# Four sets of state powers and two tap products made by GpSimd instead of VectorE, with a new issue order, in a kernel of a state-space layer beside sliding attention

## The chip, the core and the metric

The kernel runs on one core of a Trainium2 chip. The core has five engines, each with its own instruction queue: TensorE (PE; its weight loads are PEld), VectorE (DVE), ScalarE (ACT), GpSimd (POOL) and SyncE (SP), which issues nearly all DMAs. Within a queue instructions run in order; between queues they wait for each other through semaphores. The metric is the device time of one execution in microseconds.

## What is computed

Two layers on separate inputs of 2048 tokens x 448 channels, their outputs side by side in 896 columns of bf16:

```python
# A: diagonal state-space layer, P = 448 complex states
Lam_bar = exp(dt * Lam);  B_bar = ((Lam_bar - 1) / Lam)[:, None] * Bmat
Bu = einsum("bld,pd->blp", x, B_bar)
for t in range(L):
    h = Lam_bar * h + Bu[:, t]
y = 2 * einsum("blp,dp->bld", hseq, Cmat).real + x * Dskip
# B: attention of 16 heads x 28 channels over W = 8 earlier tokens, 2 apart
q, k, v = split(x @ wqkv)
attn = softmax(where(mask, einsum("bhsd,bhswd->bhsw", q, kg) * Dh**-0.5, -1e9))
o = einsum("bhsw,bhswd->bhsd", attn, vg);  out = o @ wo
```

## The kernel before

**Layout.** Token 16 p + j sits in partition p at position j: every partition holds 16 consecutive tokens. What the text calls "tokens 0 to 7" are the positions j = 0 to 7 of every partition, block b = 0; positions 8 to 15 are block b = 1. Each block has two halves of four positions, r = 1 (the upper) and r = 0. Work goes from b = 1 to b = 0 and from r = 1 to r = 0.

**Part A** (class PartA). The 448 complex states are seven sets m of 64, real and imaginary parts in 128 rows. The recurrence is done as matrix products: the input products (PE, L1247 and L1256), then steps that multiply by powers of Lam_bar (PE, L1266 to L1304, a scan over chunks), then the carries back to all tokens (L1311 to L1350), each followed by an eviction from PSUM by ScalarE. The powers of one set are 15 matrices, block-diagonal, in one tile "pw" of 128 x 1920 bf16. `powers` (L1190) builds it with one product of VectorE (L1197): a mask "Dm" times the small table "spair", both spread out by broadcasting. There are four pw buffers for seven sets: set m from 4 on can be built only after the last use of set m - 4 (the unit done[m - 4], after L1350). Then the outputs: y = C h + D x (PE, L1458 and L1462), an eviction (`outputs`, L1463 on) and a DMA to the output. For the last four positions D x is made by VectorE (`load_skip`, L1439) and added in the eviction (L1474).

**Part B** (class PartB). Projections of q and k (L481, L488, L514) and of v (L753, L760); logits as products on VectorE (L654, L656, L660: tile "prods") summed over each head's channels by PE (L672, L678); softmax (L701 to L722); a DMA transposition of the attention weights. Then `pv`: for each block b and half r, four tap pairs i = 0 to 3, each a product of weights and values over 2 taps x 4 positions x 448 channels = 3584 elements on VectorE (`mul`, L819; the first straight into the sum, tile "rb", the others into the three "prods" buffers, tap pair 3 into the third), three additions (`add`, L822) and the sum of the two taps of the pair (L838, or in two parts L841 for the very last half). The sum goes through a transposition (SP, L872, or PE, L884, for the last half) to the output projection (PE, L900, L908, L915), an eviction by ScalarE and a DMA.

**Order.** The program first lists its work as 685 units (`Planner.add`): engine, cost, function, units it depends on, buffers. An entry may name two engines. `ORDER` then gives the sequence in which all units are issued, as a flat list of unit numbers, 1000 more where the unit runs on the second of its engines. If the list's length is not that of the units, the planner makes a sequence itself from costs and priorities. Each engine gets its instructions in that sequence, so `ORDER` fixes what stands behind what on every queue. The engines wait only for data and buffers, wherever a unit stands in the list.

**Units that matter here** (numbers of before): 221, 260, 299, 338, 373, 412, 449 are the power sets m = 0 to 6; 533 to 540 are `pv` for b = 1 and 571 to 579 for b = 0. In each half the four units are: products 0 and 1; product 2 and addition 1; product 3 and addition 2; addition 3 and the sum of the taps. On POOL's queue stand, after the setup, only four memsets of the first row of v's halo (L778), of 0.7 us each.

Of the kernel before, what the change touches and what calls it, by code (L numbers as in the profile page):

```python
# [10 lines left out]
ALU = mybir.AluOpType  # L11
# [7 lines left out]
NCH = 128  # L19
# [20 lines left out]
NC = 3  # L40
# [6 lines left out]
ADD = (0, 0, 0, 0, 0, 0, 0)  # L47
EADD = (0, 0, 0, 0)
# [272 lines left out]
class PartB:  # L321
# [464 lines left out]
    def pv(self, b, prio, deps):  # L786
# [13 lines left out]
        lasts, halves, trs = {}, {}, {}  # L800
        for r in (1, 0):
            last = getattr(self, "pv_last", None)
            half = getattr(self, "u_half", None)
            ahead = half is not None
            us = (5, 4, 1, 0)
            for n in range(4):

                def step(n=n, r=r, part=0, half=half):
# [4 lines left out]
                    def mul(i):  # L813
                        u = us[i]
                        o = j0 + 4 * r + DIL * u
                        w0 = 4 * (u // 4) + 2 * (u % 2)
                        aa = self.attn[b][:, w0:w0 + 2, :, r, :].rearrange("q y i h -> q (y i) h").unsqueeze(2).to_broadcast(
                            [NCH, 8, DH, H])
                        V.tensor_tensor(tmp[i].rearrange("p (j d h) -> p j d h", j=8, d=DH), aa, self.vd[:, o:o + 8], op=ALU.mult)  # L819
# [3 lines left out]
                    if n == 0:  # L823
                        mul(1 if half else 0)
                        mul(2 if half else 1)
                    elif n == 1 and half:
                        mul(3)
                        mul(0)
                    elif n == 2 and half:
                        add(1)  # L830
                        add(2)
                    elif n < 3:
                        mul(n + 1)
                        add(n)
                    elif 2 * b + r > 0:
                        add(3)
                        if not EADD[2 * b + r]:
                            V.tensor_tensor(acc[:, n1:2 * n1], acc[:, 0:n1], acc[:, n1:2 * n1], op=ALU.add)  # L838
# [4 lines left out]
                for u in us[:2 + ahead] if n == 0 else us[n + 1 + ahead:n + 2 + ahead] if n < 3 else ():  # L843
# [3 lines left out]
                cost = 2 * vec2(2 * n1) if n < 3 else vec2(2 * n1) + vec2(n1) * (not EADD[2 * b + r]) if 2 * b + r > 0 else vec2(n1)  # L847
                last = P.add("DVE", cost, step, dd + [self.u_attn[b], last, *self.u_prod[0], *self.u_prod[1], *self.u_lg[0], *self.u_lg[1],
                                         *self.u_vm, *self.u_proj, *deps, half if n == 1 else None], prio - 0.1 * r)
# [5 lines left out]
            g = 2 * b + r  # L855
            halves[g] = self.u_half = None
            if EADD[g]:

                def merge(g=g):
                    acc = self.acc[g]  # L860
                    nc.gpsimd.dma_start(acc[:, n1:2 * n1], acc[:, 0:n1], accum_op=ALU.add)
                halves[g] = self.u_half = P.add("POOL", 1.1, merge, [last], PRI["wo"], lat=3.5)
            if not hasattr(self, "u_first"):
                self.u_first = last
        for r in (1, 0):
            g = 2 * b + r
            if g > 0:
# [5 lines left out]
                trs[r] = P.add("SP", 1.7, trd, [halves[g] or lasts[r][1]], PRI["wo"], lat=3.6)  # L873
# [70 lines left out]
class PartA:  # L944
# [245 lines left out]
    def powers(self, m, prio, deps):  # L1190
# [4 lines left out]
        def build():  # L1195
            t = pool.tile([NCH, 2 * NPW, 32, 2], bf16, name="pw", tag="pw", bufs=4)
            V.tensor_tensor(t[:], self.o["Dm"][:].rearrange("p (a b) -> p a b", b=2).unsqueeze(1).to_broadcast(  # L1197
# [5 lines left out]
        u = P.add("DVE", vec2(2 * NPW * PL), build, [self.u_s, *deps], prio, acq="pw")  # L1203
        return box, u

    def scan(self, prio, qk_done):
# [9 lines left out]
        for m in range(NM):  # L1216
# [99 lines left out]
            def carry(out, lt, Sc, hv, new=False):  # L1316
                mt(out[:, 0:NCH], lhsT=lt, rhs=Sc, start=new, stop=True, **kw)
# [13 lines left out]
            def again(n, box=box, pair=pair):  # L1331
# [5 lines left out]

# [4 lines left out]
            def s6(box=box, Sc=Sc, L=L, hget=hget, again=again, add=bool(ADD[m])):  # L1342
                if add:
                    again(0)
# [254 lines left out]
```

## Time and profile before

| | |
|---|---|
| Time, two runs | 140.18 and 140.28 us, median 140.23 |
| The profiled execution | 140.0 us, of which the span from the first to the last instruction is 138.3 us |
| Granted TensorE clock, mean | 0.997 |
| VectorE, products of `pv` (L819) | 16 x 2.02 us, of them 12 into "prods" |
| VectorE, additions of `pv` (L822) | 11 x 2.02 us |
| VectorE, power sets (L1197) | 7 x 1.15 us, the first at 19.9, the last at 85.5 us |
| GpSimd, all | 69 instructions, 17.7 us; the last ends at 33.1 us |
| DMA | 16.58 MB, mean 120 GB/s |

How to read what follows: "128x3584 bf16<-128x3584 bf16" is the output and the first input, partitions x elements. In a line of the timeline stand start, duration, engine, line and operation; consecutive instructions of one line are merged ("x3"). In a line of groups stand the count, the busy time in all, the mean duration in ns, and the idle time of the engine before them with what ended it. The chain of waits follows the work that ended last back to the start; its durations run to the next step, not to the instruction's own end. An "SPq" is the issue of a DMA by SP. Durations on POOL are rough.

### The profile page before, as it was taken

To read this page: it belongs to the slowest core of one execution; us is meant where nothing else is said; L and a number is where in the kernel's file an instruction comes from. 1 tells how busy PE (TensorE), PEld (TensorE's weight loads), DVE (VectorE), ACT (ScalarE), POOL (GpSimd) and SP (SyncE) were. 2 spreads that over 40 slices of the span, in tenths; PEclk is the share of its full clock that TensorE was granted. 3 is DMA by queue.
4 is the path that set the end of the run, shared out by engine and by line. 5 is a ranking of instruction groups with operands and counts; after the bars stand their busy time and mean duration, and the time that the engine had idled before them with its cause. 6 is when DMAs were issued, how large, how long until landed. Compare 5 with 4: busy or idle time off the path is not lost.

```text
span 138.3 us, 2835 instructions
## 1 busy us (share of the span) xinstructions
PE 131.3 (95%) x1065; PEld 67.2 (49%) x1071; DVE 123.0 (89%) x134; ACT 88.3 (64%) x199; POOL 17.7 (13%) x69
## 2 busy tenths in 40 slices
PE   7999989999999999999999999999999999999790
PEld 2534334444455453656534563556565455445450
DVE  1369998899999999997999999999999999999920
ACT  3555587998554976657695998689547151721571
POOL 7589830025000000000000000000000000000000
PEclk9999999999999999999999999999999999999998
DMA  4968965658658525648899039350093425575163
GB/s 128 269 126 208 179 87 61 153 130 95 81 113 53 97 52 112 179 104 131 167 222 198 0 67 240 95 111 0 0 95 103 139 78 118 141 163 169 35 197 100
DMA packets 41694, 16.58 MB, mean 120 GB/s; under 512 B 33685, under 2 KB 41044, under 8 KB 41681
## 3 DMA queue, kind: packets, MB, share of 16 engines
q1 hardware_dynamic: 41618, 16.40, 57.6%
q8 instruction: 8, 0.13, 0.4%
q14 instruction: 5, 0.04, 0.1%
q10 hardware_dynamic: 63, 0.01, 0.0%
HBM read 4.32 MB, written 3.67 MB: 58 GB/s over the span
## 4 chain that ended last, share of the span: by engine, by line
DVE 39%; PE 38%; SPq 9%; issue 5%; ACT 3%; DMA 3%; DVEq 0%; ACTq 0%
DVE rb L822 11%; DVE prods L819 11%; SPq L366 6%; PE v_ps L760 6%; PE scb L1247 5%; DVE rb L819 4%; PE scp L1247 4%; PE logits L672 3%; DMA rb<-in_B_x_dram 3%; DVE pw L1197 2%; PE qk_ps L481 2%; DVE prods L656 2%; PE wo_ps L915 2%; DVE rb L838 2%; ACT qk L218 1%
## 5 line engine op out<-in xcount | busy, mean ns | idle before, releaser
L819 DVE TENSOR_TENSOR prods<-attn,vd 128x3584 bf16<-128x3584 bf16 x12 | 24.0, 2018 | 0.0
L822 DVE TENSOR_TENSOR rb<-rb,prods 128x3584 bf16<-128x3584 bf16 x11 | 22.2, 2019 | 0.1
L656 DVE TENSOR_TENSOR prods<-qk 128x3072 bf16<-128x3072 bf16 (+1 forms) x15 | 19.1, 1325 | 0.0
L481 PE MATMUL qk_ps<-rb 128*128 128x512 bf16 x60 | 14.4, 379 | 0.7 <-DMA rb<-in_B_x_dram 0.6
L1462 PE MATMUL y_ps<-Ccat,qk 128*128 128x448 bf16 x60 | 14.6, 352 | 0.0
L218 ACT CAST vd<-v_ps 128x448 bf16<-128x448 f32 x16 | 7.9, 540 | 5.2 <-PE v_ps L760 4.9
L1247 PEld LDWEIGHTS <-Bcat 128*128 128x128 bf16 x84 | 7.5, 100 | 7.4 <-issue 1.1
L1294 ACT CAST ubuf<-scb 128x64 bf16<-128x64 f32 x35 | 7.3, 220 | 5.9 <-PE scb L1301 3.5
L218 ACT CAST qk<-wo_ps 128x448 bf16<-128x448 f32 (+1 forms) x16 | 8.1, 529 | 4.5 <-PE wo_ps L908 2.8
L1462 PE MATMUL y_ps<-Ccat,h 128*128 128x448 bf16 x45 | 11.0, 353 | 0.0
L1247 PE MATMUL scb<-xaT_sb,Bcat 128*128 128x512 bf16 x42 | 10.9, 380 | 0.0
L218 ACT CAST qk<-y_ps 128x448 bf16<-128x448 f32 (+1 forms) x9 | 5.6, 663 | 8.2 <-issue 4.2
L760 PE MATMUL v_ps<-rb 128*128 128x448 bf16 x48 | 10.1, 353 | 0.0
L220 ACT ACTIVATE qk<-qk_ps 64x512 bf16<-64x512 f32 (+1 forms) x15 | 8.9, 599 | 1.7 <-PE qk_ps L488 1.3
L481 PEld LDWEIGHTS <-rb 128*128 128x128 bf16 x60 | 5.6, 98 | 7.8 <-issue 1.0
L660 DVE TENSOR_TENSOR prods<-qk 128x768 bf16<-128x768 bf16 (+3 forms) x18 | 9.1, 566 | 0.1
L1462 PEld LDWEIGHTS <-qk 128*128 128x128 bf16 x60 | 5.8, 98 | 5.3 <-ACT qk L1364 0.2
L819 DVE TENSOR_TENSOR rb<-attn,vd 128x3584 bf16<-128x3584 bf16 x4 | 8.1, 2021 | 0.1
L908 PE MATMUL wo_ps<-wo_p,rb 128*128 128x448 bf16 x36 | 8.1, 353 | 0.0
L1197 DVE TENSOR_TENSOR pw<-Dm,spair 128x1920 bf16<-128x1920 bf16 x7 | 8.1, 1150 | 0.0
L218 ACT CAST qk<-qk_ps 128x512 bf16<-128x512 f32 (+2 forms) x11 | 6.3, 585 | 2.5 <-PE qk_ps L488 1.1
L1247 PE MATMUL scp<-xaT_sb,Bcat 128*128 128x512 bf16 x30 | 7.8, 381 | 0.0
(197 smaller groups left out, 259.0 us busy)
## 6 DMA issues: line engine op xcount, KB each, us to landing
out_dram<-qk SPq DMA_DIRECT2D x32, 112.0 KB, 1.8
vd<-vd SPq DMA_DIRECT2D x3, 392.0 KB, 4.5
rb<-in_B_wqkv_dram SPq DMA_DIRECT2D x3, 336.0 KB, 4.5
qk<-in_A_x_dram SPq DMA_DIRECT2D x1, 448.0 KB
ra<-in_A_B_re_dram SPq DMA_DIRECT2D x1, 392.0 KB, 4.3
ra<-in_A_B_im_dram SPq DMA_DIRECT2D x1, 392.0 KB
rb<-in_A_C_re_dram SPq DMA_DIRECT2D x4, 98.0 KB, 2.9
rb<-in_A_C_im_dram SPq DMA_DIRECT2D x4, 98.0 KB, 3.5
```

The lines of the kernel that those rows point to most:

```text
L218: nc.scalar.copy(out, in_)
L220: nc.scalar.mul(out, in_, scale)
L366: nc.sync.dma_start(self.xT[:, j], bass.AP(x.tensor, x.offset + j * D - DT, [[T * D, NCH], [1, KT * NCH]]), transpose=True)
L481: nc.tensor.matmul(out(n), lhsT=w(n, full, k), rhs=self.xT[:, j:j + 4, k, :], start=(not rfirst and k == 1), stop=(rfirst and k == KT - 1) ...
L656: V.tensor_tensor(out.rearrange("p i j k q -> p i (j k) q"), qq.unsqueeze(1).to_broadcast([NCH, 2, 4 * nk, NCH]), bass.AP(kk.tensor, kk.of ...
L660: V.tensor_tensor(jk(out[:, i, a:e]), qq, kk, op=ALU.mult)
L760: nc.tensor.matmul(box["ps"][:].rearrange("p h d -> p (h d)"), lhsT=self.xT[:, j, k, :], rhs=self.wv[:, k, :], start=False, stop=(k == KT ...
L819: V.tensor_tensor(tmp[i].rearrange("p (j d h) -> p j d h", j=8, d=DH), aa, self.vd[:, o:o + 8], op=ALU.mult)
L822: V.tensor_tensor(acc, acc, tmp[i], op=ALU.add)
L1197: V.tensor_tensor(t[:], self.o["Dm"][:].rearrange("p (a b) -> p a b", b=2).unsqueeze(1).to_broadcast([NCH, 2 * NPW, 32, 2]), self.sp[:, m ...
L1247: mt(box[i], lhsT=self.Bcat[:, k, m, :], rhs=self.xk(slice(i, None, 4), k), start=(i % 2 == 0 and k == 0), stop=False, **kw)
L1462: nc.tensor.matmul(ps, lhsT=h, rhs=self.Ccat[:, m, :], start=(m == 0 and not skip), stop=(m == NM - 1), skip_group_check=True)
```

## The change

1. `powers`: the unit may run on VectorE or GpSimd. In the new `ORDER` sets 0 to 2 stay on VectorE, and 3, 4, 5 and 6 run on GpSimd.
2. `pv`: the product of tap pair 3 becomes a unit of its own (n = 4, listed ahead of the other four of its half), for VectorE or GpSimd. In the new `ORDER` the two of b = 1 stay on VectorE, the two of b = 0 run on GpSimd. Addition 3 waits for it. The other units are then: products 0 and 1; product 2 and addition 1; addition 2; addition 3 and the sum of the taps. There are four units more, 689, and the new list has 689 numbers.
3. `ORDER` is another list from the last loads of A's x on; up to there it is the same. In it, three evictions of v (positions 7, 10, 12), one copy of A's x rows (i = 2, L1005) and two evictions of y (positions 7 and 10) run on VectorE instead of ScalarE. On VectorE the skip multiply (L1439) and the first of the three L1474 now stand ahead of the last three units of `pv`; in before they stood behind them. On SP the two loads for the skip multiply stand together behind the first output of y (before: one some twenty issues ahead of the other), the fourth halo copy of v goes ahead of the transposing load of C, and the output DMAs have another sequence. On POOL two of the four memsets stay ahead of the power sets; one follows set 3, one set 6; behind that come the two tap products.
4. Two options that were off in before (sums added by DMA: `ADD`, `EADD`, with `NC`) are taken out of the code. The instructions they would have made did not exist.

```diff
-            for n in range(4):
+            for n in (4, 0, 1, 2, 3):
...
-                        V.tensor_tensor(tmp[i].rearrange("p (j d h) -> p j d h", j=8, d=DH), aa, self.vd[:, o:o + 8], op=ALU.mult)
+                        (V if eng == "DVE" else nc.gpsimd).tensor_tensor(
+                            tmp[i].rearrange("p (j d h) -> p j d h", j=8, d=DH), aa, self.vd[:, o:o + 8], op=ALU.mult)
...
                     if n == 0:
-                        mul(1 if half else 0)
-                        mul(2 if half else 1)
...
+                        mul(0)
+                        mul(1)
+                    elif n == 4:
+                        mul(3)
                     elif n < 3:
-                        mul(n + 1)
+                        if n == 1:
+                            mul(2)
                         add(n)
...
+                c = vec2(2 * n1)
+                cost = (2 * c, 2 * c, c, (c + vec2(n1)) if 2 * b + r > 0 else vec2(n1), (c, 9.8))[n]
...
+                if n == 4:
+                    third = P.add(("DVE", "POOL"), cost, lambda e, f=step: f(eng=e), dd, prio - 0.1 * r, until=0.0)
+                else:
+                    last = P.add("DVE", cost, step, dd + [third if n == 3 else None], prio - 0.1 * r)
...
-        def build():
+        def build(eng):
             t = pool.tile([NCH, 2 * NPW, 32, 2], bf16, name="pw", tag="pw", bufs=4)
-            V.tensor_tensor(t[:], self.o["Dm"][:].rearrange("p (a b) -> p a b", b=2).unsqueeze(1).to_broadcast(
+            (V if eng == "DVE" else nc.gpsimd).tensor_tensor(t[:], self.o["Dm"][:].rearrange("p (a b) -> p a b", b=2).unsqueeze(1).to_broadcast(
...
-        u = P.add("DVE", vec2(2 * NPW * PL), build, [self.u_s, *deps], prio, acq="pw")
+        u = P.add(("DVE", "POOL"), (vec2(2 * NPW * PL), 5.2), build, [self.u_s, *deps], prio, acq="pw", until=0.0)
...
 ORDER = [
...
-    145, 142, 146, 149, 144, 23, 188, 189, 125, 169, 127, 179, 490, 126, 491, 493, 505, 132, 130, 492, 485, 486,
+    145, 142, 146, 149, 144, 132, 125, 127, 188, 189, 126, 505, 515, 184, 516, 518, 506, 508, 185, 177, 519,
...
+    303, 286, 250, 251, 1338, 252, 253, 255, 257, 287, 288, 254, 292, 526, 256, 258, 215, 532, 293, 525, 305,
+    216, 307, 306, 308, 259, 1373, 289, 290, 309, 294, 296, 291, 339, 340, 341, 342, 310, 295, 297, 343, 345,
...
+    409, 544, 440, 464, 465, 441, 445, 442, 444, 466, 467, 402, 403, 404, 446, 468, 633, 469, 470, 577, 1578,
```

More of the change, by code (lines that the diff above doesn't have):

```diff
@@ L799, in pv, with step @@
         self.oTd = getattr(self, "oTd", {})
-        lasts, halves, trs = {}, {}, {}
+        lasts, trs = {}, {}
         for r in (1, 0):
             last = getattr(self, "pv_last", None)
-            half = getattr(self, "u_half", None)
-            ahead = half is not None
             us = (5, 4, 1, 0)
-            for n in range(4):
-                def step(n=n, r=r, part=0, half=half):
+            for n in (4, 0, 1, 2, 3):
+                def step(n=n, r=r, part=0, eng="DVE"):
                     alloc()
@@ L842, in pv @@
                 dd = []
-                for u in us[:2 + ahead] if n == 0 else us[n + 1 + ahead:n + 2 + ahead] if n < 3 else ():
+                for u in us[:2] if n == 0 else us[2:3] if n == 1 else us[3:] if n == 4 else ():
                     o = j0 + 4 * r + DIL * u
@@ L846, in pv @@
                         dd += self.u_vh[p] if p < HALO else [self.u_v[p - HALO]]
-                cost = 2 * vec2(2 * n1) if n < 3 else vec2(2 * n1) + vec2(n1) * (not EADD[2 * b + r]) if 2 * b + r > 0 else vec2(n1)
-                last = P.add("DVE", cost, step, dd + [self.u_attn[b], last, *self.u_prod[0], *self.u_prod[1], *self.u_lg[0], *self.u_lg[1],
-                                         *self.u_vm, *self.u_proj, *deps, half if n == 1 else None], prio - 0.1 * r)
+                c = vec2(2 * n1)
+                cost = (2 * c, 2 * c, c, (c + vec2(n1)) if 2 * b + r > 0 else vec2(n1), (c, 9.8))[n]
+                dd += [self.u_attn[b], last, *self.u_prod[0], *self.u_prod[1], *self.u_lg[0], *self.u_lg[1], *self.u_vm, *self.u_proj, *deps]
+                if n == 4:
+                    third = P.add(("DVE", "POOL"), cost, lambda e, f=step: f(eng=e), dd, prio - 0.1 * r, until=0.0)
+                else:
+                    last = P.add("DVE", cost, step, dd + [third if n == 3 else None], prio - 0.1 * r)
             lasts[r] = [last, last]
@@ L1314, in ev3, with carry @@
                 nc.scalar.copy(hget()[:, 3, 0:384], box[3][:, 0:384])
-            def carry(out, lt, Sc, hv, new=False):
-                mt(out[:, 0:NCH], lhsT=lt, rhs=Sc, start=new, stop=True, **kw)
+            def carry(out, lt, Sc, hv):
+                mt(out[:, 0:NCH], lhsT=lt, rhs=Sc, start=False, stop=True, **kw)
                 mt(out[:, NCH:512], lhsT=lt, rhs=hv[:, 3, 0:384], start=False, stop=True, **kw)
@@ L1329, in ev1f, with back @@
                 nc.scalar.copy(hget()[:, 1, :], box[1])
-            def again(n, box=box, pair=pair):
+            def back(n, box=box, pair=pair, hget=hget):
                 if pair and n == 0:
@@ L1403, in scan @@
             b0 = b2 = eh
-            add = bool(ADD[m])
-            if not hold[0] and not add:
+            if not hold[0]:
                 b0 = P.add("PE", pe(1, 512), lambda f=back: f(0), [b0], PRI["bk"] + m * 0.1, acq="W" if pair else "s")
-            if not hold[pair ^ 1] and not add:
+            if not hold[pair ^ 1]:
                 b2 = P.add("PE", pe(1, 512), lambda f=back: f(1), [b2, b0], PRI["bk"] + m * 0.1, acq=None if pair else "s")
-            v0 = P.add("PE", pe(2, 256), s6, [b0, u3], pc, acq=("W" if pair else "s", "cP") if add else None)
-            v2 = P.add("PE", pe(1, 512), s7, [b2, u1, v0 if add and pair else None], pc, acq="s" if add and not pair else None)
+            v0 = P.add("PE", pe(2, 256), s6, [b0, u3], pc)
+            v2 = P.add("PE", pe(1, 512), s7, [b2, u1], pc)
             if pair:
```

52 lines of the change are left out of this document (11 added, 41 removed), and 45 rows, old and new, of the table ORDER.

## The prediction

> **What bounds the kernel now.** I read the page first, then the windows, then VectorE's timeline and the chain, and last GpSimd's rows, since the change moves work from the one to the other.
>
> ```profile
> PE 131.3 (95%) x1065; PEld 67.2 (49%) x1071; DVE 123.0 (89%) x134; ACT 88.3 (64%) x199; POOL 17.7 (13%) x69
> POOL 7589830025000000000000000000000000000000
> DVE 39%; PE 38%; SPq 9%; issue 5%; ACT 3%; DMA 3%; DVEq 0%; ACTq 0%
> ```
>
> Two engines share the chain about evenly, and POOL does nothing after the tenth of 40 slices. The windows (busy time of PE, PEld, DVE, ACT and POOL in each stretch) show whether the two take turns or are full together:
>
> ```profile
> 18.00:44.00 26.00, 25.60 (x263) 12.61 (x264) 24.69 (x33) 19.80 (x39) 3.41 (x6) 1.00 0.65 101
> 64.00:80.00 16.00, 15.76 (x108) 8.02 (x109) 15.93 (x10) 12.73 (x36) 0.00 (x0) 1.00 0.72 142
> 90.00:126.00 36.00, 35.90 (x255) 19.69 (x256) 35.79 (x20) 19.43 (x44) 0.00 (x0) 1.00 0.45 100
> 128.50:138.30 9.80, 5.54 (x45) 3.30 (x45) 3.59 (x6) 4.99 (x10) 0.00 (x0) 0.96 0.37 117
> ```
>
> From 90 to 126 us PE is busy 35.90 and VectorE 35.79 of 36 us. Neither has room: what lengthens VectorE's work there lengthens the kernel, and what shortens it alone meets a full PE. The profiled execution took 140.0 us, 1.7 more than its span of 138.3, and 0.23 under the median of 140.23; I count against 140.0.
>
> **The change part by part.** *Removed from VectorE.* Four power sets (m = 3 to 6) and the last product of r = 1 and of r = 0 for tokens 0 to 7. Their rows in VectorE's timeline, and in the chain (which counts start to start, so without the overlap with the next instruction):
>
> ```profile
> 49.41 1.15 DVE L1197 TENSOR_TENSOR pw<-Dm,spair 128x1920 bf16<-128x1920 bf16 x1
> 68.52 1.15 DVE L1197 TENSOR_TENSOR pw<-Dm,spair 128x1920 bf16<-128x1920 bf16 x1
> 80.58 1.15 DVE L1197 TENSOR_TENSOR pw<-Dm,spair 128x1920 bf16<-128x1920 bf16 x1
> 85.52 1.15 DVE L1197 TENSOR_TENSOR pw<-Dm,spair 128x1920 bf16<-128x1920 bf16 x1
> 107.58 2.02 DVE L819 TENSOR_TENSOR prods<-attn,vd 128x3584 bf16<-128x3584 bf16 x1
> 122.50 2.02 DVE L819 TENSOR_TENSOR prods<-attn,vd 128x3584 bf16<-128x3584 bf16 x1
> 85.60 1.07 DVE pw L1197
> 83.67 1.94 DVE prods L819
> ```
>
> 4 x 1.07 + 2 x 1.94 = 8.2 us less on VectorE.
>
> *Added to GpSimd.* No such size ran there. Its nearest rows are products of two float32 operands:
>
> ```profile
> L1081 POOL TENSOR_TENSOR karg<-kv,arg 128x105 f32<-128x105 f32 x1 | 0.4, 362 | 0.0
> L1124 POOL TENSOR_TENSOR cs<-sh 128x210 f32<-128x210 f32 x1 | 0.5, 539 | 0.0
> ```
>
> 105 elements more cost 177 ns, 1.69 ns each. So 1920 elements take 3.2 us and 3584 take 6.0 us, beside about 0.2 us of fixed cost: 4 x 3.2 + 2 x 6.0 = 24.8 us. The lower end is half of it (bf16 is half the bytes): 12.4 us. The upper end is the price that the code's planner has for the two, 5.2 and 9.8 us: 40.4 us. I take 24.8, the only one with a measured slope behind it.
>
> *Do the two engines run beside each other?* This decides the sign. In the only place where a GpSimd instruction that reads SBUF met one of the large products of VectorE:
>
> ```profile
> L1129 POOL TENSOR_SCALAR la<-la,turn x2: 499/788/1078, 14.3 to 14.8; 128x7 f32<-128x7 f32 x2
> 14.31 1.57 POOL L1129 TENSOR_SCALAR la<-la,turn 128x7 f32<-128x7 f32 x2
> 14.36 0.29 DVE L222 COPY rb<-rb 64x512 bf16<-64x512 bf16 x1
> 14.68 0.96 DVE L654 TENSOR_TENSOR prods<-qk 128x1536 bf16<-128x1536 bf16 x1
> L1127 POOL TENSOR_TENSOR la<-cs,ex 128x14 f32<-128x14 f32 x1 | 0.2, 238 | 0.1
> ```
>
> Twice the same 7 elements: 499 and 1078 ns, where 14 elements took 238 ns just before. The first ends at 14.81, 0.16 after VectorE's copy (14.65); the second at 15.88, 0.24 after VectorE's product (15.64). Both look as if GpSimd stood still until VectorE had finished. If so the two exclude each other, and it matters little who goes first: a GpSimd product of 3.2 us needs 3.2 us in which VectorE runs no product, and between 90 and 126 us VectorE leaves 0.2 us free. For the other direction there is only a hint: of three small products of VectorE beside GpSimd work, the one that began 0.03 us after a GpSimd instruction took 0.12 us longer than its like, and another was not slowed at all:
>
> ```profile
> 8.01 0.15 DVE L1108 TENSOR_TENSOR t<-pf 128x7 f32<-128x7 f32 x1
> 8.16 0.50 POOL L1086 TENSOR_SCALAR kf<-kf 128x105 f32<-128x105 f32 x1
> 8.19 0.27 DVE L1109 TENSOR_TENSOR den<-den,t 128x7 f32<-128x7 f32 x1
> 8.75 0.50 POOL L1091 TENSOR_SCALAR kc<-kf 128x105 f32<-128x105 f32 x1
> 8.93 0.17 DVE L1114 TENSOR_TENSOR ll<-pf,rden 128x14 f32<-128x14 f32 x1
> ```
>
> The Trainium skill speaks against this change: "SBUF — State Buffer", section "Who interferes with whom", has a VectorE instruction with two SBUF inputs and a GpSimd instruction that reads SBUF exclude each other, the one that starts first holding the port for the whole instruction. By that rule the sum is the one I make below. The trace agrees for VectorE's hold (1078 ns above); no row shows GpSimd's.
>
> The skill's "GPSIMD Engine Reference", section 3.1, gives 4497 ns for a float32 product of 2048 elements, at which the six would take about 4 x 4.2 + 2 x 7.9 = 32.6 us (an estimate from that page), and the sum below would be 7.8 us more.
>
> So on VectorE: 24.8 added less 8.2 removed, **+16.6 us**; ends 12.4 - 8.2 = +4.2 and 40.4 - 8.2 = +32.2; and -8.2 if the two do not disturb each other at all.
>
> *Evictions moved from ScalarE to VectorE*: three of v's (j = 7, 10, 12) and the copy of A's x rows for i = 2; two of y's (j = 7, 10) come at the very end.
>
> ```profile
> L222 DVE CAST qk<-qk_ps 128x512 bf16<-128x512 f32 (+1 forms) x9 | 6.1, 688 | 0.5 <-POOL kc L1093 0.3
> L222 DVE COPY rb<-rb 64x512 bf16<-64x512 bf16 (+1 forms) x3 | 0.8, 268 | 0.9 <-DMA rb<-in_B_wqkv_dram 0.8
> ```
>
> 448 of 512 columns: 0.60 us, so 3 x 0.60 + 0.27 = **+2.1 us** on a full VectorE. ScalarE, at 64%, gains nothing that counts.
>
> *The tail.* After the last adds of tokens 0 to 3 the chain now runs:
>
> ```profile
> 127.49 1.10 DVE rb L841
> 129.49 0.45 PE pt_o L884 x8
> 130.32 1.62 DVE qk L1474 x2
> 131.98 0.61 PE pt_o L884 x8
> 132.59 2.28 PE wo_ps L915 x12
> 134.94 0.53 ACT qk L218
> ```
>
> The new order puts the skip multiply (L1439) and the first of the three L1474 ahead of the last adds; two L1474 still follow. The stretch of the chain that hangs on L1474, from 129.94 (where L884 x8 ends) to 131.98, can go: **-2.0 us**; at worst 0.
>
> *Waits and queues.* PE's first product with a GpSimd set (L1266) waits for GpSimd, with all of PE's queue behind it. There is room:
>
> ```profile
> 64.75 0.38 PE L1350 MATMUL scp<-h,pw 128*128 128x512 bf16 x1
> 76.79 0.40 PE L1266 MATMUL scb<-qk,pw 128*128 128x512 bf16 x1
> 30.32 2.82 POOL L778 MEMSET vd<- 1x896 f32 x4 [11.68 <-ACT qk L218]
> ```
>
> Set 4 takes set 0's buffer, free after 64.75, and is needed at 76.79: 12 us for a product of 3.2 (5.2 at most). Set 3 needs no buffer and starts behind two of the four memsets, near 30.32 + 1.4 = 31.7. VectorE's third addition (L822) waits for the last product; behind it on VectorE stand the half sums, and for them wait SP's transposition (L872) and PE's output projection. The buffer comes free with the previous block's third addition; from there to its own there are a half sum and five 1.94 us steps, 10.8 us: room for 6.0, barely for 9.8. The memset left behind set 6 (halo rows 2 to 5) and the other transfers that change places on SP's queue have POOL's and SP's idle time around them: nothing.
>
> *Sum.* 140.0 + 16.6 + 2.1 - 2.0 = 156.7. Set 3 falls where PE, not VectorE, carries the chain:
>
> ```profile
> 35.30 2.38 PE v_ps L760 x12
> 39.43 2.38 PE v_ps L760 x12
> ```
>
> so I count its net 3.2 - 1.07 = 2.1 us as half hidden: **forecast 155.6 us**. This case's own ends are 144 (12.4 us of GpSimd work) and 172 (40.4 us).
>
> **The rivals.** *They run side by side, and PE bounds.* For it: L1114 above, and that GpSimd is idle when it gets the work. Against it: L1129. VectorE would be 8.2 - 2.1 = 6.1 us shorter, but PE can only close its own gaps: 0.8 us between 128.5 and 134.9 (5.54 busy of 6.4; after that there is only eviction and output), 0.1 from 90 to 126, 0.2 from 64 to 80, 0.4 from 18 to 44, and as much again in gaps that the modelled matmul ends cover. That is 1.5 to 3 us: 137 to 138.5. It decides if GpSimd's products leave VectorE's steps at 1.94 us. The little that lies beyond 2% needs nearly all of these gaps.
>
> *They share the port finely.* GpSimd reads bf16 in pairs and takes only 12.4 us from VectorE: 140.0 + 4.2 + 2.1 - 2.0 = 144. For it: half the bytes per element. Against it: the whole-instruction wait of L1129.
>
> *VectorE always wins, GpSimd starves.* Then set 4 to 6 come late and PE stops; the six products still need their 24.8 us of free port, so it ends near the forecast, with the stops on PE instead.
>
> That the order list is not used is excluded: 685 + 4 new units are 689, as many as it has numbers.
>
> **How the numbers follow.** They exclude each other, either winner: 0.45, 155.6 us. Fine sharing: 0.15, 144. Side by side: 0.40, 137 to 138.5 and in part up to 140, of which 0.15 beyond 2%. A measurement of this kernel tells about 2% (2.8 us) from no change. Faster 0.15; same 0.25; slower 0.45 + 0.15 = 0.60. The range 137 to 163 leaves out some 0.10 below and 0.10 above (GpSimd at the planner's price). Within the likeliest case alone it is 146 to 163.
>
> **What would show it.** Right: VectorE's steps at L819 and L822 near GpSimd's six products grow from 2.0 to 5 us or more, or GpSimd's products last 5 us or more and end just behind a VectorE instruction; VectorE's busy time grows, PE's windows from 64 us on fall below 90%. Wrong: L819 and L822 keep 2.02 us in all their rows while GpSimd's L1197 runs; VectorE's busy time falls to about 117 us and PE's share rises. The eviction term is wrong if ScalarE, not VectorE, ends the waits before 60 us; the tail term if L1474 still stands between L841 and the last L884.

## The result and the profile after

| | before | after |
|---|---|---|
| Time, median of two runs | 140.23 us | 166.45 us (166.12 and 166.78) |
| Ratio to before, 95% interval | | 1.187 (1.177 to 1.197) |
| Span of the profiled execution | 138.3 us | 165.0 us |
| Last adds of tokens 0 to 3 end, by VectorE's timeline | 128.57 us | 153.29 us |

The kernel became 18.7% slower: slower as forecast, but 10.9 us beyond the forecast of 155.6 and 3.5 us beyond the upper end of the range. Lines have moved in the code: `powers` is now L1185, the products of `pv` are L814, its additions L818, the half sums L830 and L833, the skip multiply L1409, the sums with y L1444.

The page after, busy time of the engines:

```profile
PE 140.6 (85%) x1065; PEld 69.7 (42%) x1071; DVE 145.0 (88%) x134; ACT 86.0 (52%) x193; POOL 48.9 (30%) x75
```

VectorE was relieved of six products and yet is busy 22 us longer, at the same share of a longer span. Which of its instructions grew is in the groups by line and shape (count, then busy time and mean ns of one):

```profile
L814 DVE TENSOR_TENSOR prods<-attn,vd 128x3584 bf16<-128x3584 bf16 x10 | 29.5, 2980 | 0.0
L814 DVE TENSOR_TENSOR rb<-attn,vd 128x3584 bf16<-128x3584 bf16 x4 | 21.3, 5324 | 0.1
L818 DVE TENSOR_TENSOR rb<-rb,prods 128x3584 bf16<-128x3584 bf16 x11 | 22.2, 2019 | 0.3
```

The products' means hide a few very long ones; the additions (L818) still take 2.02 us. VectorE's timeline after (start, duration) shows them, each where a GpSimd product runs:

```profile
30.09 10.09 DVE L653 TENSOR_TENSOR prods<-qk 128x3072 bf16<-128x3072 bf16 x5
41.29 0.62 DVE L219 CAST vd<-v_ps 128x448 bf16<-128x448 f32 x1 [1.10 <-PE v_ps L757]
...
72.72 10.37 DVE L814 TENSOR_TENSOR prods<-attn,vd 128x3584 bf16<-128x3584 bf16 x2
...
87.00 5.26 DVE L814 TENSOR_TENSOR prods<-attn,vd 128x3584 bf16<-128x3584 bf16 x1
...
111.54 1.09 DVE L830 TENSOR_TENSOR rb<-rb 128x1792 bf16<-128x1792 bf16 x1
112.67 8.65 DVE L814 TENSOR_TENSOR rb<-attn,vd 128x3584 bf16<-128x3584 bf16 x1
...
132.47 8.61 DVE L814 TENSOR_TENSOR rb<-attn,vd 128x3584 bf16<-128x3584 bf16 x1
...
146.81 1.08 DVE L1409 TENSOR_TENSOR qk<-qk,rb 128x1792 bf16<-128x1792 bf16 x1
148.08 1.09 DVE L1444 TENSOR_TENSOR qk<-y_ps,qk 128x896 bf16<-128x896 f32 x1 [0.19 <-issue]
149.08 2.02 DVE L818 TENSOR_TENSOR rb<-rb,prods 128x3584 bf16<-128x3584 bf16 x1
151.20 2.09 DVE L833 TENSOR_TENSOR rb<-rb,prods 128x1792 bf16<-128x1792 bf16 x2
```

GpSimd's timeline, the same stretches:

```profile
32.30 3.39 POOL L1185 TENSOR_TENSOR pw<-Dm,spair 128x1920 bf16<-128x1920 bf16 x1
...
71.47 4.60 POOL L1185 TENSOR_TENSOR pw<-Dm,spair 128x1920 bf16<-128x1920 bf16 x1 [34.99 <-PE scp L1331]
...
111.64 7.79 POOL L814 TENSOR_TENSOR prods<-attn,vd 128x3584 bf16<-128x3584 bf16 x1 [20.49 <-DVE rb L818]
131.39 7.81 POOL L814 TENSOR_TENSOR prods<-attn,vd 128x3584 bf16<-128x3584 bf16 x1 [11.95 <-DVE rb L818]
```

Read the first tap product. GpSimd's record starts at 111.64, while VectorE's half sum runs until 112.63. GpSimd ends at 119.43. VectorE's next product is in hand from 112.67 and ends at 121.32; it needs 2.02 us, so it ran from 119.30. Read so, GpSimd stood 1.0 us until VectorE's instruction was over, then held VectorE for 6.7 us, and it got its turn ahead of a VectorE instruction that followed at once. The sets bear this out: the record of set 4 (from 71.47, 4.60 us) is 1.2 us longer than that of set 6 (from 86.98, 3.41 us), and VectorE's instruction that was running then had 1.34 us to go for set 4 (until 72.81) and 0.10 us for set 6 (until 87.08). The two engines take turns, one instruction at a time.

The windows after (busy time of PE, PEld, DVE, ACT and POOL in each stretch, then granted clock) show what this did to TensorE, which had been nearly full up to 126 us:

```profile
31.00:44.00 13.00, 9.46 (x104) 4.02 (x103) 11.86 (x11) 4.19 (x9) 5.42 (x5) 0.74 0.48 91
80.00:100.00 20.00, 12.61 (x97) 6.54 (x96) 19.79 (x11) 9.51 (x30) 5.39 (x3) 0.82 0.26 54
150.00:165.00 15.00, 11.57 (x76) 6.34 (x74) 5.77 (x8) 5.47 (x10) 0.00 (x0) 0.84 0.43 138
```

TensorE's longest wait is for no product at all, but for a 0.15 us cast of the skip weights, which VectorE reached only at 97.30 us, behind the holds of sets 4 to 6 (85.30 us in run e1_order below, where TensorE does not wait for it):

```profile
PE scb L1244 <- DVE dsk L1054: 7.1, 1, 7.1
```

**The account, by VectorE's timeline.** Stretch: set 3 3.8 us (10.09 against 6.29 for the same five products in run e2_taps below), sets 4 and 5 6.4 (10.37 against 3.95), set 6 3.2 (5.26 against 2.02), the two tap products 6.6 each (8.65 and 8.61 against 2.02): 26.7 us. Removed products: -8.2. Three evictions of v and a copy ahead of the last adds: +2.1. The skip multiply and one sum with y, now ahead of the last two steps (146.81 to 149.08): +2.3. Together 22.9 of the 24.7 us by which the last adds end later; the other 1.8 were not followed one by one, but the 1.10 us for TensorE at 41.29, behind set 3, is among them. From the last adds to the end of the span it takes 11.7 instead of 9.7 us: +2.0.

The end itself does not hang on these adds. The chain that ended last goes from the skip multiply and the first sum with y straight to TensorE:

```profile
148.08 1.10 DVE qk L1444
...
149.22 0.53 PE y_ps L1428 x4
...
154.48 0.45 PE pt_o L872 x8
...
161.60 0.53 ACT qk L215
```

TensorE had waited 4.5 us for this sum. From 149.22 to 161.58 us it then works without a pause, and it comes to the transpositions of the last adds' result (L872) 1.2 us after these have ended.

### The profile page after: what moved, and what is told of

It reads as the page before. It is cut to its first block, busy times and chain, and to the rows that moved or that the text cites. A ratio compares the mean times of both kernels' runs of the same rounds, so it can differ in the third digit from the quotient of the medians.

```text
span 165.0 us, 2839 instructions
## 1 busy us (share of the span) xinstructions
PE 140.6 (85%) x1065; PEld 69.7 (42%) x1071; DVE 145.0 (88%) x134; ACT 86.0 (52%) x193; POOL 48.9 (30%) x75
## 5 line engine op out<-in xcount | busy, mean ns | idle before, releaser
L814 DVE TENSOR_TENSOR prods<-attn,vd 128x3584 bf16<-128x3584 bf16 x10 | 29.5, 2980 | 0.0
L1185 POOL TENSOR_TENSOR pw<-Dm,spair 128x1920 bf16<-128x1920 bf16 x4 | 15.7, 3936 | 41.6 <-PE scp L1331 35.8
L814 POOL TENSOR_TENSOR prods<-attn,vd 128x3584 bf16<-128x3584 bf16 x2 | 15.6, 7802 | 32.4 <-DVE rb L818 32.4
L653 DVE TENSOR_TENSOR prods<-qk 128x3072 bf16<-128x3072 bf16 (+1 forms) x15 | 23.0, 1579 | 0.3 <-PE logits L669 0.3
L818 DVE TENSOR_TENSOR rb<-rb,prods 128x3584 bf16<-128x3584 bf16 x11 | 22.2, 2019 | 0.3
L814 DVE TENSOR_TENSOR rb<-attn,vd 128x3584 bf16<-128x3584 bf16 x4 | 21.3, 5324 | 0.1
L215 ACT CAST qk<-wo_ps 128x448 bf16<-128x448 f32 (+1 forms) x16 | 8.3, 526 | 24.6 <-PE wo_ps L896 18.7
L1432 PE MATMUL y_ps<-Ccat,qk 128*128 128x448 bf16 x60 | 16.8, 388 | 0.1
L1282 ACT CAST ubuf<-scb 128x64 bf16<-128x64 f32 x35 | 7.0, 218 | 12.9 <-PE scb L1289 10.1
L1432 PE MATMUL y_ps<-Ccat,h 128*128 128x448 bf16 x45 | 12.6, 394 | 0.0
L757 PE MATMUL v_ps<-rb 128*128 128x448 bf16 x48 | 11.7, 401 | 0.0
L1244 PE MATMUL scb<-xaT_sb,Bcat 64*128 64x512 bf16 x14 | 3.2, 391 | 7.1 <-DVE dsk L1054 7.1
L1289 PEld LDWEIGHTS <-pw 128*128 128x128 bf16 x63 | 4.3, 108 | 11.2 <-issue 9.0
```

What stands on the lines that cost most here:

```text
L215: nc.scalar.copy(out, in_)
L653: V.tensor_tensor(out.rearrange("p i j k q -> p i (j k) q"), qq.unsqueeze(1).to_broadcast([NCH, 2, 4 * nk, NCH]), bass.AP(kk.tensor, kk.of ...
L757: nc.tensor.matmul(box["ps"][:].rearrange("p h d -> p (h d)"), lhsT=self.xT[:, j, k, :], rhs=self.wv[:, k, :], start=False, stop=(k == KT ...
L814: (V if eng == "DVE" else nc.gpsimd).tensor_tensor(tmp[i].rearrange("p (j d h) -> p j d h", j=8, d=DH), aa, self.vd[:, o:o + 8], op=ALU.mult)
L818: V.tensor_tensor(acc, acc, tmp[i], op=ALU.add)
L1185: (V if eng == "DVE" else nc.gpsimd).tensor_tensor(t[:], self.o["Dm"][:].rearrange("p (a b) -> p a b", b=2).unsqueeze(1).to_broadcast([NCH ...
```

## Experiments

The theory: a GpSimd product that reads SBUF and a VectorE product with two SBUF inputs exclude each other, and the sum above is what that costs. Rivals: the new order, not GpSimd, costs the time (e1); GpSimd's results or its writes, not its reading, cost it (e4); only GpSimd's two-input form does it (e6). Later runs went after the part of the time that the forecast missed. In the diffs the numbers are entries of `ORDER`, 1000 more where a unit runs on the second of its engines.

### The order alone, and each kind of product alone

e1_order (all six products on VectorE) and the parts of it that e2_taps and e3_sets leave on GpSimd:

```diff
-    1338 ... 1373 ... 1412 ... 1449 ... 1573 ... 1578      (after)
+     338 ...  373 ...  412 ...  449 ...  573 ...  578      (e1_order)
+     338 ...  373 ...  412 ...  449 ... 1573 ... 1578      (e2_taps)
+    1338 ... 1373 ... 1412 ... 1449 ...  573 ...  578      (e3_sets)
```

> The changed kernel with all six products back on VectorE; the new order and the evictions on VectorE stay. If VectorE's and GpSimd's products exclude each other and that is the whole loss: VectorE loses the 27.2 us by which its busy time was stretched and gets 8.2 us back, so 166.5 - 27.2 + 8.2 = 147 us if the end moves with it one to one, and 139 to 143 us if PE's lower clock and its idle stretches go with the stretching. If the new order is what costs: 155 us or more. If late results of GpSimd were the loss: like the first, 139 to 147, but then the two partial versions must show PE or VectorE waiting for GpSimd.

> Only the two tap products on GpSimd, the four sets back on VectorE. Exclusion: each of the two holds VectorE for about 6.8 us and saves 1.94, so 9.7 us more than the version with all on VectorE, and one VectorE instruction of about 8.6 us behind each. Order: the same time as the version with all on VectorE. Late results: VectorE's third addition (L818) waits for GpSimd; the instruction behind GpSimd's start keeps 2.0 us.

> Only the four power sets on GpSimd, the two tap products back on VectorE. Exclusion: each holds VectorE for about 3.3 us and saves 1.07, so 9 us more than the version with all on VectorE, and the two partial versions' extra times add up to what the changed kernel has above it. Order: the same time as the version with all on VectorE. Late results: PE's L1254 of sets 4 to 6 waits for GpSimd.

| run | time, us | ratio to before, 95% interval | VectorE busy, us |
|---|---|---|---|
| e1_order | 148.96 | 1.066 (1.061 to 1.070) | 126.3 |
| e2_taps | 156.07 | 1.115 (1.110 to 1.119) | 135.7 |
| e3_sets | 156.76 | 1.119 (1.116 to 1.123) | 135.7 |

Either kind of product costs 7 to 8 us more on GpSimd than on VectorE in the same order, and VectorE's busy time grows by 9.4 us in both: the stretch less the products taken off (for the taps 6.7 + 6.6 - 2 x 1.94). Both together cost 17.5 us more than e1_order. In time the expectations of 9.7 and 9 us were too high, and the two alone add up to 14.9 of the 17.5 us. VectorE's waits for y's products near the end, 6.0 us in e1_order, are 2.3 and 2.0 us here, so a part of the holds fell where VectorE had waited anyway. That the stretch does not belong to one kind of VectorE instruction shows in e2_taps, where a power set came behind GpSimd's first tap product; GpSimd's rows, then VectorE's:

```profile
100.24 7.67 POOL L814 TENSOR_TENSOR prods<-attn,vd 128x3584 bf16<-128x3584 bf16 x1 [65.60 <-DVE rb L818]
```

```profile
101.06 7.86 DVE L1185 TENSOR_TENSOR pw<-Dm,spair 128x1920 bf16<-128x1920 bf16 x1
108.84 2.01 DVE L814 TENSOR_TENSOR rb<-attn,vd 128x3584 bf16<-128x3584 bf16 x1
```

This set was the one that TensorE waited for: its wait is 12.7 us here, against 6.1 us in e1_order.

The surprise was e1_order: 8.9 us slower than before without any GpSimd product. Its waits name the place:

```profile
PE scb L1254 <- DVE pw L1185: 6.1, 1, 6.1
ACT e L1258 <- PE scb L1254: 8.4, 3, 6.5
```

Set 6 stands late in the new list, which does not matter to an idle GpSimd; on VectorE it was made at 100.55 us, 15 us later than in before, and TensorE waited 6.1 us for it.

### What about GpSimd's work hurts

e4_memset lets GpSimd write the same tiles for as long, without reading SBUF:

```diff
-            nc.gpsimd.tensor_tensor(tile, ..., op=ALU.mult)
+            for _ in range(2):
+                nc.gpsimd.memset(tile, 0.0)
```

> The six GpSimd products are replaced by two memsets each of the same tile, which read nothing (sets 3 to 6 and the two tap products are left out and stand at zero); GpSimd is busy for about 2 x 1.9 and 2 x 3.6 us in the same places, and VectorE is relieved as in the change. If only the reading of the two engines excludes: no VectorE instruction is stretched (L814 and L818 at 2.02 us throughout) and the time is what the offload would have brought without contention, by PE's gaps 136 to 140 us. If any GpSimd work beside VectorE costs: 150 us or more.

138.55 us, ratio 0.989 (0.986 to 0.992). Its groups by line (here the products are L818, the additions L822):

```profile
L822 DVE TENSOR_TENSOR rb<-rb,prods 128x3584 bf16<-128x3584 bf16 x11 | 22.2, 2021 | 0.3
L818 DVE TENSOR_TENSOR prods<-attn,vd 128x3584 bf16<-128x3584 bf16 x10 | 19.9, 2018 | 0.0
...
L1191 POOL MEMSET pw<- 128x1920 bf16 x8 | 13.6, 1698 | 38.1 <-PE scp L1339 31.2 <-PE scP L1339 6.6
L816 POOL MEMSET prods<- 128x3584 bf16 x4 | 12.3, 3085 | 18.4 <-DVE rb L822 18.3
```

GpSimd works 25.9 us beside VectorE in the same places, and no product of VectorE is longer than 2.03 us. So neither the writes nor the semaphores do it: what excludes VectorE's products is the reading. It also shows the most that this offload could bring in this order: with six products gone from VectorE and nothing in return, the kernel is 1.1% faster; TensorE is then busy for 97% of the span.

e6_onein asks whether one input is enough, with a copy in the place of each product:

```diff
-            nc.gpsimd.tensor_tensor(tile, in0, in1, op=ALU.mult)
+            nc.gpsimd.tensor_scalar(tile, in0, 1.0, None, op0=ALU.mult)
```

> The six GpSimd products become copies through a multiplication by 1.0, which read one SBUF tensor instead of two (the second factor is left out in sets 3 to 6 and in the two tap products). If any reading by GpSimd excludes VectorE's products: VectorE instructions behind them are stretched by the length of the copies, about 1.7 to 2 us for a set and 3.2 to 4 us for a tap product, 13 to 16 us in all, and the time is 150 to 155 us. If only two-input GpSimd products do: no stretching and 138 to 140 us, as with the memsets.

169.27 us, ratio 1.207, slower than with the products, and beyond the 150 to 155 us expected, for which the copies had been put at 2 and 4 us at most. GpSimd's groups, then a row of VectorE's timeline:

```profile
L1190 POOL TENSOR_SCALAR pw<-Dm 128x1920 bf16<-128x1920 bf16 x4 | 21.8, 5456 | 36.5 <-PE scp L1339 32.5 <-PE scP L1339 4.0
L815 POOL TENSOR_SCALAR prods<-vd 128x3584 bf16<-128x3584 bf16 x2 | 20.3, 10135 | 30.1 <-issue 19.0 <-DVE rb L822 11.1
```

```profile
112.72 10.10 DVE L818 TENSOR_TENSOR rb<-attn,vd 128x3584 bf16<-128x3584 bf16 x1
```

One input excludes as well: VectorE was held for 8.1 us (10.10 less the 2.02 it needs). And the copy takes longer than the product it replaces (10.1 against 7.8 us).

### Which VectorE instructions are held

Two probes put small instructions on VectorE ahead of the stretched product, into GpSimd's hold. e7_probe:

```diff
+                            V.memset(self.scr[:], 0.0)
+                            V.tensor_reduce(self.scr2[:], self.scr[:], axis=AX.X, op=ALU.max)
                         mul(0)
```

> The changed kernel with two more VectorE instructions ahead of the first product of each half of block b = 0, where GpSimd's tap product holds: a memset of 1024 elements (no SBUF input) and a maximum over them (one SBUF input). If only a second SBUF input is shut out: both run at their own 1.1 to 1.3 us inside GpSimd's 7.8 us, the product behind them is stretched by the rest, about 4.3 us instead of 6.6, and the time stays within 1 us of 166.5. If every VectorE instruction is shut out: the first of them takes 7 us or more, and the time is about 4 us more.

e10_copy adds a packed copy between the two:

```diff
                             V.memset(self.scr[:], 0.0)
+                            V.tensor_copy(self.scr3[:], self.scr[:].rearrange("p a b -> p (a b)"))
                             V.tensor_reduce(self.scr2[:], self.scr[:], axis=AX.X, op=ALU.max)
```

> The changed kernel with the memset and the reduction of the earlier probe, and between them a copy of 1024 bf16 elements from SBUF to SBUF on VectorE (one input, but in the fast packed form: the 512-column copy took 0.29 us, so about 0.55 us alone), ahead of the products of tokens 0 to 7 and so inside GpSimd's hold. If every VectorE instruction with one SBUF input passes, the copy takes about 0.55 us, the product behind it is stretched to about 6.4 us and the time stays near 166.4. If the packed copy needs the shared port too, as the Trainium skill (SBUF, section on who interferes with whom) has it for copies in the two-port modes, the copy takes some 6 us and ends at GpSimd's end, the reduction and the product behind it take 1.2 and 2.0 us, and the time grows by about 1.8 us per place, to some 169 to 171.

166.38 and 170.41 us (one execution each). VectorE's timeline in e7_probe, then in e10_copy:

```profile
112.28 0.48 DVE L824 MEMSET probe<- 128x512 uint32 x1
112.80 1.22 DVE L825 TENSOR_REDUCE probed<-probe 128x128 bf16<-128x1024 bf16 x1
113.94 6.97 DVE L814 TENSOR_TENSOR rb<-attn,vd 128x3584 bf16<-128x3584 bf16 x1
```

```profile
113.10 0.48 DVE L825 MEMSET probe<- 128x512 uint32 x1
113.62 6.51 DVE L826 COPY copied<-probe 128x1024 bf16<-128x1024 bf16 x1
120.06 1.20 DVE L827 TENSOR_REDUCE probed<-probe 128x128 bf16<-128x1024 bf16 x1
121.19 2.01 DVE L814 TENSOR_TENSOR rb<-attn,vd 128x3584 bf16<-128x3584 bf16 x1
```

Memset and reduction pass through the hold: the reduction takes 1.22 us in it and 1.20 us behind it (e10_copy). They cost the kernel nothing; the product behind them waits for the same end. The packed copy has one input too, and is held like a product: 6.51 us. Then everything behind it moves out of the hold, and two places cost 4 us, as the second theory had it. The Trainium skill, "SBUF — State Buffer", section "Who interferes with whom", states both halves: a VectorE instruction with at most one SBUF input does not contend, except in the modes that use both ports, which copies can enter; a product with two inputs contends with GpSimd's reads but not with its writes. The trace agrees in every case tried: 0.48 and 1.22 us passing, 6.51 and 6.97 us held, 2.02 us beside memsets.

### The old order with four sets on GpSimd

e8_before_sets takes the kernel before, with its evictions and its tail, and moves sets 3 to 6 alone:

```diff
-    338 ... 373 ... 412 ... 449
+    1338 ... 1373 ... 1412 ... 1449
```

> The kernel before, its order kept, with sets 3 to 6 alone on GpSimd. Exclusion: each set holds VectorE for about 3.3 us and saves 1.07 us, so up to 9 us more than 140: 145 to 149, less where a hold falls on evictions from PSUM. If the loss came only with the new order: 138 to 141.

The two executions took 150.99 and 153.48 us, 10.8 and 13.3 us above before, more than the 5 to 9 us expected; the profile is that of the longer one. In it VectorE's busy time grew by 9.2 us (123.0 to 132.2), about what the forecast had for the sets (4 x 3.2 - 4.3 = 8.5), and VectorE is idle 4.3 us longer. TensorE's longest wait is the one seen in the changed kernel:

```profile
PE scp L1340 <- DVE dsk L1066: 8.0, 1, 8.0
```

The 0.15 us cast of the skip weights stands on VectorE behind three holds, at 94.03 us instead of 80.51, and TensorE's whole queue stands behind it. So a hold can cost more than its own length, through small results that are queued behind it; how much of the time above VectorE's 9.2 us this wait makes was not separated.

### What the new order costs without GpSimd

Starting from e1_order, one edit at a time: e5_set6 issues set 6 (unit 449) among the products where before has it; e9_evict also gives the six moved evictions back to ScalarE; e11_tail also puts the last 77 units into before's sequence.

```diff
-    540, 541, 542, 449, 450, 572,
+    219, 34, 449, 423, 563,                       (e5_set6: moved up)
-    1507 ... 1150 ... 1492 ... 1497 ... 1631 ... 1676
+     507 ...  150 ...  492 ...  497 ...  631 ...  676        (e9_evict)
-    622, 680, ... 581, 582, ... 583,              (skip multiply, sum, then the adds)
+    581, 582, 583, ... 622, ... 680,              (e11_tail: the adds first)
```

> All six products on VectorE in the new order, with one step moved: set 6 stands ahead of the products of the half r = 0 of b = 1 instead of two blocks later. In the version without this step PE waited 6.1 us for set 6 (L1254 on L1185). If that misplacement is what the order alone costs: 142 to 144 us, with that wait gone. If the evictions and the moved skip multiply on VectorE are what costs: 147 to 149 us, as without the step.

> The new order with all six products on VectorE and set 6 in its old place (145.22 us), and now also the six evictions that the change moved to VectorE (three of v, the copy of A's x, two of y) given back to ScalarE at the same places of the order. If the 5 us left over the kernel before are these evictions on a full VectorE (its busy time was 126.3 us against 123.0), VectorE's busy time goes back to about 123 us and the time to 141 to 142.5. If the rest is the new order itself (which token block's products stand where, and the adds behind them), VectorE gets 3.3 us shorter but the time stays at 144 to 145. If both engines needed the move because ScalarE was late, it gets slower than 145.2.

> The run before (new order, all six products and the six evictions where the kernel before has them, set 6 in its old place: 145.07 us, VectorE busy 123.4 us), and now also the last 77 units of the order in the sequence of the kernel before: the last adds of tokens 0 to 3 again ahead of the skip multiply and of the sums with y, and y of tokens 2 and 6 ahead of that of 12 and 13. If the new tail is what costs (the skip multiply and one sum hold the last adds back by 2.4 us, and the stretch behind the adds is 1.1 us longer), the time falls by 2 to 3.5 us, to 141.5 to 143. If it is the time that TensorE lost before (busy 17.9, 19.1 and 8.0 us in the stretches 80 to 100, 100 to 120 and 120 to 130 us, against 20.0, 20.0 and 9.4), its work still has to be done at the end, whatever stands first there, and the time stays at 144 to 145.5. If my forecast's tail term held (the new tail saves 2.0 us), it gets slower, to 146.5 or more.

| run | time, us | ratio to before, 95% interval |
|---|---|---|
| e1_order | 148.96 | 1.066 (1.061 to 1.070) |
| e5_set6 | 145.22 | 1.036 (1.034 to 1.037) |
| e9_evict | 145.07 | 1.035 (1.031 to 1.038) |
| e11_tail | 142.32 | 1.016 (1.013 to 1.020) |

Set 6's place was worth 3.7 us. The evictions are worth nothing that can be measured, although they took VectorE 2.9 us (126.3 to 123.4). The tail is worth 2.75 us, with a clear sign. The chain of waits of e9_evict shows how:

```profile
126.19 1.00 DVE qk L1409
...
127.38 1.09 DVE qk L1444
128.47 1.94 DVE rb L818
...
131.45 1.09 DVE rb L833
...
132.59 0.65 PE pt_o L872 x8
133.23 0.19 PE y_ps L1432
133.42 0.57 PE wo_ps L896 x3
133.99 1.51 PE y_ps L1432 x8
```

The skip multiply and one sum delay the last adds by 2.3 us, and the adds are what the last transpositions of TensorE wait for; y's last products still stand between these. In e11_tail the adds end 2.2 us earlier. What is left, 2.3 us above before, was not followed further: TensorE is busy 17.8 us between 80 and 100 us there, against 19.95 in before.

### The old tail in the changed kernel

e12_after_tail is the changed kernel with the same 77 units in before's sequence; e13_tail_y also returns y's two evictions (1631 and 1676) to ScalarE.

> The changed kernel (166.45 us), GpSimd's six products included, with the last 77 units of its order in the sequence of the kernel before, as in the run before. In the changed kernel the skip multiply and one sum stand 2.4 us ahead of the last adds, and the stretch behind the adds grew from 9.7 to 11.7 us. If the new tail costs what these say, the time falls by 2.4 to 4.4 us, to 162 to 164. If there the tail is free, because TensorE, behind by VectorE's stops and at a lower clock, has work left anyway, it stays at 165.5 to 167. If my forecast's tail term held, it gets slower by 2 us, to 168.5.

> The run before (changed kernel with the old tail, 166.24 us), and y's two evictions (tokens 7 and 10) on ScalarE again. In the trace of the run before TensorE stood still 6.4 us, from 141.3 to 147.65, for these two evictions: they were queued on VectorE behind the product that GpSimd's hold had stretched to 8.6 us, two more products and an addition. If this wait is what hid the gain of the old tail, the last adds end 1.1 us sooner, the wait of 6.4 us is gone, and the time falls by 2.5 to 4.5 us, to 162 to 164. If TensorE then meets another wait behind the same hold (a transposition, a buffer), or is bound by its lower clock, the time stays at 165.5 to 166.5.

166.24 us (ratio 1.189, 1.186 to 1.191) and 169.20 us (1.206, 1.201 to 1.211). Neither gives the 2.75 us. TensorE's waits from 125 us on, in the changed kernel, in e12_after_tail and in e13_tail_y:

```profile
PE y_ps L1428 <- DVE qk L1444: 4.5, 1, 4.5
PE wo_ps L888 <- DMA rb<-rb: 3.7, 1, 3.7
```

```profile
PE wo_ps L888 <- DVE qk L219: 6.4, 1, 6.4
```

```profile
PE y_ps L1432 <- DVE qk L1444: 8.8, 1, 8.8
```

Each sequence has TensorE waiting for something that VectorE does behind the last hold: a sum, an eviction, then a sum again. The theory that the one wait of 6.4 us hid the gain falls: with that wait gone a longer one took its place, and the time is outside both expectations. TensorE has its instructions in the same sequence in e11_tail and e13_tail_y; why it waits for the sum in the one and not in the other is open.

No run of the whole computation beat the kernel before. The experiments point to none either: in the new order relief of VectorE is worth 1.1% at most, and what could pay for it on GpSimd would have to avoid reading SBUF. What the relief alone would bring in the old order was not tried.

## Why the prediction was right, and where it was wrong

- **Exclusion, either winner** (0.45): right, shown by e4_memset against the changed kernel and by the probes. The forecast had seen only VectorE's hold; the runs show GpSimd's.
- **Holds, 24.8 us**: measured 26.7. The slope of two float32 rows gave the sets to the digit (3.2 us for sets 4 to 6; 3.8 for set 3) and the taps a tenth low (6.0 against 6.6). That float32 rows of 105 and 210 elements fit bf16 products so closely is in part luck: no run has the same product in both types. The 4497 ns that stand beside them are, in the Trainium skill's "GPSIMD Engine Reference", section 3.1, those of an addition; the 32.6 us worked out from them lie above the 26.7 measured.
- **Removed, 8.2 us**: right; VectorE's busy time fell by 7.8 us from e1_order to e4_memset.
- **Evictions, +2.1 us**: right as VectorE's work (2.9 us with y's), wrong as time without GpSimd's products: nothing measurable in e9_evict. In the changed kernel it was not tried.
- **Tail, -2.0 us**: the step that failed, in sign. I let "the stretch of the chain that hangs on L1474" go, at worst for nothing, and overlooked that what is moved out of it goes in front of the adds. No run shows the 2.0 us. Without GpSimd's products the new tail costs 2.75 us (e11_tail): skip multiply and sum put the adds 2.3 us back, and the chain passes both (e9_evict). In the changed kernel undoing it gave nothing (166.24 against 166.45 us). There VectorE does not carry the end to its last adds, as the forecast had it: TensorE, late by its waits behind the holds, waits 4.5 us for the sum and then has 12.4 us of work left. By VectorE's timeline the adds came 2.3 us later and the stretch behind them grew by 2.0 us instead of shrinking by 2.0: 6.3 of the 10.9 us missed. How these 6.3 us divide between the tail and TensorE's lateness stays open.
- **The new order as a whole**: with tail and evictions I had it at 2.1 - 2.0 = +0.1 us. Without GpSimd's products it costs 8.9 us (e1_order), and 5.0 with set 6 in its old place (e5_set6). Counted from there GpSimd's products cost 21.2 us, where I had 16.6 - 1.05. This divides the excess otherwise than VectorE's timeline does, and no run decides between the two: with VectorE relieved and not held (e4_memset) the same order costs nothing.
- **Set 3 half hidden, -1.05 us**: wrong. TensorE's busy time in the stretch from 31 to 44 us fell to 9.46 of 13.00 us (12.94 in before), and VectorE then waited 1.10 us for it: nothing hid the hold.
- **Waits and queues**: right that no engine would wait for GpSimd's results; in the changed kernel's list of waits no engine waits for one. What I left out is the reverse: results that wait on VectorE behind a hold (7.1 us for the cast and 4.5 us for the sum in the changed kernel, 8.0 us in e8_before_sets).
- **Side by side** (137 to 138.5 us): refuted, but its price was close: 138.55 us when GpSimd does not read.
- **VectorE always wins**: refuted. GpSimd gets its turn at the next instruction boundary.
- **The range**: its upper end of 163 has no sum of its own. The holds and set 3 alone would have stayed inside it (1.9 and 1.05 us); it left the tail at 0 at worst and had nothing for results that wait behind a hold.

By VectorE's timeline, then, the excess is 6.3 us around the last adds, 1.9 in the holds, 1.05 in set 3, and most of the rest waits of VectorE.

## What to carry to other kernels

Before moving elementwise work from VectorE to GpSimd, ask what VectorE runs meanwhile: if both read SBUF as these do, a GpSimd product takes its whole length out of VectorE, here about three times what VectorE needed for it. Count with each hold the small results queued behind it that TensorE waits for. And when work is moved out of the tail, look where it lands: ahead of the last step on the same engine it delays that step by its whole length. Check also which engine will carry the end: here it was no longer the one whose work had been counted.

## What the runs showed of the hardware beyond that

- GpSimd's copy with a scalar (one input) is slower than its product of two inputs: 10.1 against 7.8 us for 3584 elements, waits on VectorE included in both. The Trainium skill, "GPSIMD Engine Reference", section 4.1, has one-input work at about line rate and two-input work slower; these rows are the other way round.
- In e6_onein GpSimd's copy for set 6 is on record from 86.70 to 91.95 us, but VectorE's product beside it (from 86.96, 5.35 us) needs 2.02 us and so ran from 90.29 us on; beside the tap copies it ran in the last 1.0 us of their records. So the hold of a copy ends before its record does, if GpSimd's rough durations can be trusted that far.
- Writes are not harmless to everything: beside a 0.83 us memset of GpSimd (30.04 us) a copy of VectorE that began at 30.01 us (128x8, L578) took 0.91 us; in e1_order, where it began 0.21 us ahead of the memset, 0.19 us. The five products behind it were not delayed: 6.29 us in e4_memset, which has the same pair, as in e1_order.
- The granted clock was lower in the stretches in which TensorE had been stopped for 3.5 and 7.1 us (0.74 from 31 to 44 us, 0.82 from 80 to 100 us; 1.00 in both stretches of before), and it was 0.84 in the last 15 us. In e9_evict, where TensorE stood still for 2.0 us between 80 and 100 us, it stayed at 1.00. TensorE's busy time rose from 131.3 to 140.6 us with the same number of matmuls. How much of the 2.0 us behind the last adds is the clock was not separated.
